# Projections of an attention and expert kernel on quarters of TensorE's array instead of halves

## The chip, the cores and the metric

One core of a Trainium2 chip runs one program. The metric is the time of one execution on the device in microseconds (us). TensorE is called PE below, its weight loads PEld; VectorE is DVE, ScalarE ACT, GpSimd POOL, and SP the engine that issues most transfers.

## The reference

Two layers, cut to what matters. Attention with exponential features (8 batches, 8 heads, 576 positions, 64 dimensions, 128 features), then a routed mixture of 8 experts over the 4608 rows that it gives:

```
def phi(x):                                       # x: batch, head, 576, 64
    proj = einsum('bhsd,df->bhsf', x, w_phi)      # 64 -> 128 features
    proj = proj - max(abs(proj), axis=-1)
    return concatenate([exp(proj), exp(-proj)], -1)
q_p, k_p = phi(q), phi(k)
kv = einsum('bhsf,bhsd->bhfd', k_p, v);  z = sum(k_p, axis=2)
num = einsum('bhsf,bhfd->bhsd', q_p, kv)
den = einsum('bhsf,bhf->bhs', q_p, z) + 1e-06
x = (num / den)                                   # as 4608 rows of 512
logits = x @ w_gate + modality_bias[modality_id]
e = argmax(logits);  gate = softmax(logits)[e]
out = gate * (relu(x @ w1[e]) @ w2[e])
```

The change touches only the product `x @ w_phi` in `phi`.

## The kernel before

**Attention.** The 64 pairs of batch and head are worked in 16 groups of four (`qi` 0 to 15). A group's keys lie in the tile `kt`, 128 partitions of which 64 hold one head and 64 another; its queries lie likewise in `qt`. `w_phi` lies twice in the tile `wp`, once in each half of the partitions. All products here are 4-byte floats, and in the trace each such matmul shows as two records (two passes over its columns), each with a weight load (LDWEIGHTS) of its own.

The projections are made in three helpers of the class Attention, each a sequence of stages:
- `k` (line 461, twice a group): main positions of the keys. Eight matmuls, four times a pair for `a` = 0 and 1, take 64 rows of the array and all 128 columns: weights are 64x128 of `kt`, 128 columns of `wp` move past them. The result goes to the PSUM tile `pk`, of which DVE then takes maxima (line 464) and differences (467), and ACT exponentials (471).
- `e` (lines 481 and 484, once a group): the last 64 positions of the keys and of the queries, four matmuls of 128 moving columns, into two tiles `pe`.
- `q` (line 507, twice a group): main positions of the queries. Two matmuls with `wp` as weights and 512 moving columns, into `pq`. ACT, POOL (an all-reduce over partitions, line 515), DVE and ACT follow.

In the profile these carry the form 64*128 (rows times columns of the array). The two of a pair lie on different halves of the rows and run side by side.

The other products of attention have other forms: `v` sums keys times values into `kvT` on 128*32 (line 534) and its last positions on 64*64 (line 540: four matmuls of 256 moving columns, one on each quarter); `z`, `num` and `den` use 128*32 (575, 592, 599); transposes use 128*128 (554, 581, 674, 683, 692, 698).

**Order.** A list `ORDER`, written by hand, says which stage of which helper of which group comes next; each engine gets its instructions in that order. There are two PSUM buffers of two banks for projections (`pk`, `pq`) and four banks (`pm`) for all else. Loads of later groups are issued when the first stages of K, Q and E have read the tiles.

**Experts.** The class Experts gathers rows (`xg`), transposes them (798), and multiplies with weights that are loaded (`raw`), and split into two parts by ACT (788) and DVE (790): lines 825 and 842. The first of these matmuls stands among the last stages of attention; the last projection stands some 30 us ahead of them.

Of the kernel before, what the change touches and what calls it, by code (L numbers as in the profile page):

```python
# [15 lines left out]
AX = mybir.AxisListType  # L16
PSUM = bass.MemoryType.PSUM
SP, PE, ACT, DVE, POOL = (getattr(mybir.EngineType, e) for e in ("SP", "PE", "Activation", "DVE", "Pool"))

P = 128  # L20
S = 576
# [50 lines left out]
class Route:  # L72
# [28 lines left out]
    def fetch(self, mod, bias):  # L101

        nc, w = self.nc, self.w
        m2 = w.tile([P, NT, 2], I32, name="m2")
        nc.sync.dma_start(m2, mod.bitcast(I32).rearrange("p (t w) -> p t w", w=2))
        bb = w.tile([P, 2, E], F32, name="bb")
        nc.sync.dma_start(bb, bias.rearrange("m e -> (m e)").partition_broadcast(P).rearrange("p (m e) -> p m e", m=2))
        self.raw = m2, bb
# [55 lines left out]
    def group(self, lg, b, pm):  # L164
# [23 lines left out]

        rk = pm.tile([P, 512], F32, tag="pm", name="rk" + n)
        of = self.oh.rearrange("p t e -> p (t e)")  # L190
        for u in range(10):
            nc.tensor.matmul(rk[:, u * E:10 * E], self.one if u else self.U, of[:, 0:(10 - u) * E], start=u == 0, stop=u == 9)
# [146 lines left out]
class Attention:  # L339
# [86 lines left out]
    def load_v(self, qi, lv, vm, vt):  # L426
        nc, q, n = self.nc, self.st[qi], f"{qi}"
        q["va"] = lv.tile([P, 2, 4, P], F32, tag="va", name="va" + n)
        nc.sync.dma_start(q["va"], vm[qi])
        q["vb"] = lv.tile([P, P], F32, tag="vb", name="vb" + n)  # L430
        nc.sync.dma_start(q["vb"], vt[qi])
# [15 lines left out]
    def kp(self, qi, po):  # L447
# [2 lines left out]
            q["kp"] = po.tile([P, 9, 2, 2, P], F32, tag="kp", name=f"kp{qi}")  # L450
        return q["kp"]

    def k(self, qi, u, po, w, pk):


        nc, q, n = self.nc, self.st[qi], f"{qi}_{u}"
        pp = pk.tile([P, 2, 4, P], F32, tag="pk", name="pk" + n)
        for t in range(4):
            for a in range(2):
                r = slice(64 * a, 64 * a + 64)  # L460
                nc.tensor.matmul(pp[:, a, t], q["kt"][r, 4 * u + t], self.wp[r], start=True, stop=True)
        yield
        mk = w.tile([P, 2, 4], F32, tag="mk", name="mk" + n, bufs=2)
        nc.vector.tensor_reduce(mk, pp, AX.X, ALU.max, apply_absolute_value=True)
        yield
        dk = w.tile([P, 2, 4, P], F32, tag="dk4", name="dk" + n)
        nc.vector.tensor_tensor(dk, pp, mk.unsqueeze(3).to_broadcast([P, 2, 4, P]), ALU.subtract)  # L467
        yield
        kp = self.kp(qi, po)[:, 4 * u:4 * u + 4]
        for s, sc in ((0, 1.0), (1, -1.0)):  # L470
            nc.scalar.activation(kp[:, :, :, s, :].rearrange("p t a f -> p a t f"), dk, AF.Exp, scale=sc)  # L471
        yield

    def e(self, qi, po, w, pm):


        nc, q, n = self.nc, self.st[qi], f"{qi}_2"
        pp = [pm.tile([P, 512], F32, tag="pm", name=f"pe{qi}_{a}") for a in range(2)]
        for a in range(2):
            r = slice(64 * a, 64 * a + 64)  # L480
            nc.tensor.matmul(pp[a][:, 0:P], q["kt"][r, 8], self.wp[r], start=True, stop=True)
        for a in range(2):
            r = slice(64 * a, 64 * a + 64)
            nc.tensor.matmul(pp[a][:, P:2 * P].rearrange("p (r s) -> p r s", r=2), self.wp[r], q["qt"][r, :, 512:S], start=True, stop=True)
        yield
        o = self.tail(qi)
        for h in range(2):
            nc.scalar.copy(self.d.rearrange("p (r a) s -> p r a s", a=2)[:, :, h, o:o + 64], pp[h][:, P:2 * P].rearrange("p (r s) -> p r s", r=2))  # L488
        yield
        mk = w.tile([P, 2, 2], F32, tag="me", name="me" + n, bufs=2)  # L490
        for h in range(2):
            nc.vector.tensor_reduce(mk[:, 1, h:h + 1], pp[h][:, 0:P], AX.X, ALU.max, apply_absolute_value=True)
        yield
        kp = self.kp(qi, po)
        nc.scalar.mul(mk[:, 0], mk[:, 1], -1.0)
        for s, sc in ((1, -1.0), (0, 1.0)):
            for h in range(2):
                nc.scalar.activation(kp[:, 8, h, s, :], pp[h][:, 0:P], AF.Exp, bias=mk[:, s, h:h + 1], scale=sc)
        yield

    def q(self, qi, pr, po, w, pq):

        nc, q, n = self.nc, self.st[qi], f"{qi}_{pr}"
        pp = pq.tile([P, 2, 512], F32, tag="pq", name="pq" + n)
        for a in range(2):
            r = slice(64 * a, 64 * a + 64)
            nc.tensor.matmul(pp[:, a], self.wp[r], q["qt"][r, pr, 0:512], start=True, stop=True)
        yield
        d = self.d[:, 2 * pr:2 * pr + 2]
        o = self.main(qi)  # L510
        nc.scalar.copy(d[:, :, o:o + 512], pp)
        yield
        mq = w.tile([P, 2, S], F32, tag="mq", name="mq" + n, bufs=2)
        for a in range(2):
            self.line(nc.gpsimd.partition_all_reduce(mq[:, a], d[:, a], P, bass_isa.ReduceOp.absmax))  # L515
        yield
        nc.vector.tensor_tensor(d, d, mq, ALU.subtract)  # L517
        yield
        if "qp" not in q:
            q["qp"] = po.tile([P, 4, 2, S], F32, tag="qp", name=f"qp{qi}")  # L520
        for i, sc in ((0, 1.0), (1, -1.0)):
            nc.scalar.activation(q["qp"][:, 2 * pr:2 * pr + 2, i, :], d, AF.Exp, scale=sc)  # L522
        yield
# [189 lines left out]
class Experts:  # L713
# [10 lines left out]
    def weights(self, pool, names):  # L724
        for k in names:
            self.W[k] = pool.tile([P, 4, F] if k[1] == "1" else [P, 8, D], F32R, name=k)
# [5 lines left out]
    def entry(self, oi, k, i, top):  # L732

        return self.nc.values_load(oi[0:1, i, k:k + 1], engines=[SP], min_val=0, max_val=top,
                                   skip_runtime_bounds_check_because="the plan makes it within these bounds")
# [28 lines left out]
    def rload(self, r, oi, k, layer):  # L764

        r0 = self.entry(oi, k, 1, (E - 1) * 2 * P)
        for j in range(2):
            self.nc.sync.dma_start(r[2 * layer + j], (self.w1, self.w2)[layer][ds(r0, 2 * P), :]
                                   .rearrange("(p h) c -> p h c", h=2)[:, j])
# [603 lines left out]
```

## Time and profile before

| | |
|---|---|
| time, median of 3 runs | 767.35 us (767.33 to 767.49) |
| the profiled execution | 768.2 us, of which the span shown is 766.1 us |
| PE busy | 742.2 us, 97% of the span |
| DVE busy | 547.4 us, 71% |
| ACT busy | 446.9 us, 58% |
| POOL busy | 294.6 us, 38% |

Busy is the time in which at least one instruction of an engine ran. Attention fills about the first 310 us, the experts the rest. A row of a timeline gives a group's start and the length up to the modelled end of its last matmul; since ends overlap the next group's start, the distance between two starts is the better measure of what a group costs PE.

### The profile page before, as it was taken

The page shows a single profiled execution, that of the slowest core. Times are in us where ns is not written, and L with a number is a line of the kernel's source. Part 1 is how long each engine was busy: PE and PEld are TensorE (multiplying, and loading weights), DVE is VectorE, ACT ScalarE, POOL GpSimd, SP SyncE. Part 2 cuts the span into 40 slices and gives each one's busy share as a digit, 9 for nine tenths or more (in the row PEclk, how much of TensorE's full clock was granted, in tenths as well). Part 3 has the DMA queues.
Part 4 walks back from the last instruction along what each step waited for, and adds up shares of the span by engine and source line. Part 5 has one row for each costly group of instructions (what it writes and reads, how often), then busy time and mean ns, then how long its engine had stood idle before and what let it go on. Part 6 is the DMA issues. An engine that isn't in the chain of part 4 may idle for free. (4 is left out here: it accounts for less than half of the span.)

```text
span 766.1 us, 18619 instructions
## 1 busy us (share of the span) xinstructions
PE 742.2 (97%) x7387; PEld 576.3 (75%) x7387; DVE 547.4 (71%) x832; ACT 446.9 (58%) x677; POOL 294.6 (38%) x199
## 2 busy tenths in 40 slices
PE   8899999999989999999999999999999999999996
PEld 5455655555645555888999988988988999899995
DVE  7898997888778887999765673564646546656653
ACT  5988778787767787545544453444435534554532
POOL 5455345665774884243221231132122123213212
PEclk9999999999999999999999999999999999999999
DMA  8633444447542418699667983847777947786560
GB/s 239 162 96 117 128 128 128 139 114 175 124 113 76 148 19 282 180 238 388 217 207 275 403 321 120 361 162 302 279 289 279 347 165 275 291 340 228 188 241 30
DMA packets 56180, 159.20 MB, mean 208 GB/s; under 512 B 22025, under 2 KB 24205, under 8 KB 43792
## 3 DMA queue, kind: packets, MB, share of 16 engines
q1 hardware_dynamic: 48000, 138.58, 54.2%
q0 software_dynamic: 7760, 18.93, 6.8%
q8 instruction: 62, 1.02, 0.6%
q10 hardware_dynamic: 320, 0.36, 0.2%
q14 instruction: 38, 0.31, 0.1%
HBM read 140.77 MB, written 19.55 MB: 209 GB/s over the span
## 5 line engine op out<-in xcount | busy, mean ns | idle before, releaser
L788 ACT CAST h<-raw 128x1024 fp32r<-128x1024 f32 x148 | 149.6, 1051 | 103.0 <-PE p L842 50.6
L790 DVE TENSOR_TENSOR l<-raw,h 128x1024 fp32r<-128x1024 f32 x148 | 175.6, 1221 | 46.3 <-ACT h L788 35.0
L515 POOL PARTITION_ALL_REDUCE mq<-d x64 | 143.4, 2294 | 104.3 <-ACT d L488 77.3
L825 PE MATMUL p<-xl,h 128*128 128x256 f32 x576 | 163.0, 283 | 0.9 <-issue 0.9
L825 PE MATMUL p<-xh,h 128*128 128x256 f32 x576 | 163.7, 285 | 0.0
L825 PE MATMUL p<-xh,l 128*128 128x256 f32 x576 | 163.0, 284 | 0.0
L746 POOL DMA_INDIRECT xg<-x,me x40 | 56.3, 1406 | 170.7 <-DMA me<-lst 54.2
L825 PEld LDWEIGHTS p<-xh,l 128*128 128x128 f32 x576 | 110.3, 192 | 2.8 <-issue 2.6
L825 PEld LDWEIGHTS p<-xh,h 128*128 128x128 f32 x576 | 110.3, 192 | 1.5 <-issue 1.0
L825 PEld LDWEIGHTS p<-xl,h 128*128 128x128 f32 x576 | 110.4, 192 | 0.9 <-issue 0.4
L831 DVE SCALAR_TENSOR_TENSOR hl<-p,hh 128x512 fp32r<-128x512 f32 x72 | 49.5, 689 | 84.7 <-ACT hh L829 75.1
L842 PE MATMUL p<-h,hh 128*128 128x512 f32 x272 | 104.9, 395 | 0.0
L829 ACT ACTIVATE hh<-p 128x512 fp32r<-128x512 f32 x72 | 42.8, 595 | 106.3 <-PE p L825 91.6
L842 PE MATMUL p<-h,hl 128*128 128x512 f32 x272 | 103.5, 391 | 0.0
L842 PE MATMUL p<-l,hh 128*128 128x512 f32 x272 | 103.4, 390 | 0.0
L522 ACT ACTIVATE qp<-d 128x1152 f32<-128x1152 f32 x64 | 71.1, 1163 | 14.8 <-DVE d L517 13.3
L752 POOL DMA_INDIRECT out_dram<-os,me x34 | 37.5, 1104 | 81.4 <-DVE os L883 62.7
L471 ACT ACTIVATE kp<-dk 128x1024 f32<-128x1024 f32 x64 | 64.7, 1069 | 3.8 <-DVE dk L467 3.7
L534 PE MATMUL kvT<-kp,va 128*32 128x256 f32 x1024 | 61.4, 387 | 5.3 <-DVE xs L663 2.0
L567 DVE TENSOR_TENSOR kp<-kp 128x1024 f32<-128x1024 f32 x48 | 62.7, 1313 | 0.3
L842 PEld LDWEIGHTS p<-h,hl 128*128 128x128 f32 x272 | 51.1, 188 | 10.8
L842 PEld LDWEIGHTS p<-l,hh 128*128 128x128 f32 x272 | 51.1, 188 | 10.3
(259 smaller groups left out, 1114.8 us busy)
## 6 DMA issues: line engine op xcount, KB each, us to landing
raw<-in_w_dram SPq DMA_DIRECT2D x96, 1024.0 KB
qt<-in_qT_dram SPq DMA_DIRECT2D x30, 288.0 KB
va<-in_vm_dram SPq DMA_DIRECT2D x16, 512.0 KB
x<-xs SPq DMA_DIRECT2D x32, 256.0 KB
kt<-in_kT_dram SPq DMA_DIRECT2D x15, 512.0 KB
kt<-in_kT_dram SPq DMA_DIRECT2D x16, 64.0 KB
vb<-in_vt_dram SPq DMA_DIRECT2D x16, 64.0 KB
x<-xs_l SPq DMA_DIRECT2D x8, 128.0 KB
```

Source lines behind the costliest of these rows:

```text
L471: nc.scalar.activation(kp[:, :, :, s, :].rearrange("p t a f -> p a t f"), dk, AF.Exp, scale=sc)
L515: self.line(nc.gpsimd.partition_all_reduce(mq[:, a], d[:, a], P, bass_isa.ReduceOp.absmax))
L522: nc.scalar.activation(q["qp"][:, 2 * pr:2 * pr + 2, i, :], d, AF.Exp, scale=sc)
L534: nc.tensor.matmul(pt[pr][32 * c:32 * c + 32], va[:, pr, t, 32 * c:32 * c + 32], kp[:, pr * 4 + t, c // 2, :, :], start=t == 0, stop=False ...
L567: nc.vector.tensor_tensor(kv4[:, :, t], kv4[:, :, t], kv4[:, :, u], ALU.add)
L746: g = self.nc.gpsimd.indirect_dma_start(xg, None, self.x[:rows, :], IndirectOffsetOnAxis(ix.bitcast(U32), 0), bounds_check=rows - 1, oob_i ...
L788: nc.scalar.copy(h, r)
L790: nc.vector.tensor_tensor(l, r, h, ALU.subtract)
L825: nc.tensor.matmul(pp[:, j], a[:, cc, f], b[:, cc], start=i == 0, stop=i == 11)
L829: nc.scalar.activation(self.HH[:, sl], pp, AF.Relu)
L831: nc.vector.scalar_tensor_tensor(self.HL[:, sl], pp, 0.0, self.HH[:, sl], ALU.max, ALU.subtract)
L842: nc.tensor.matmul(pp, a[:, f, tk], b[:, f], start=i == 0, stop=i == 23)
```

## The change

A new helper `quarters` takes the place of the matmul in `k`, `e` and `q`. It splits the 128 columns of the weights into two halves and issues one matmul for each, on the quarter of the array that begins at row 64a and column 64c. Each writes 64 partitions of the output instead of 128. The moving operand is the same for both. The moving columns stay as they were (128 for keys and both tails, 512 for the main queries).

```
+    def quarters(self, o, w, m, a):
+        for c in range(2):
+            self.nc.tensor.matmul(o[64 * c:64 * c + 64], w[:, 64 * c:64 * c + 64], m, start=True, stop=True, tile_position=(64 * a, 64 * c))
...
-                nc.tensor.matmul(pp[:, a, t], q["kt"][r, 4 * u + t], self.wp[r], start=True, stop=True)
+                self.quarters(pp[:, a, t], q["kt"][r, 4 * u + t], self.wp[r], a)
...
-            nc.tensor.matmul(pp[a][:, 0:P], q["kt"][r, 8], self.wp[r], start=True, stop=True)
+            self.quarters(pp[a][:, 0:P], q["kt"][r, 8], self.wp[r], a)
...
-            nc.tensor.matmul(pp[a][:, P:2 * P].rearrange("p (r s) -> p r s", r=2), self.wp[r], q["qt"][r, :, 512:S], start=True, stop=True)
+            self.quarters(pp[a][:, P:2 * P].rearrange("p (r s) -> p r s", r=2), self.wp[r], q["qt"][r, :, 512:S], a)
...
-            nc.tensor.matmul(pp[:, a], self.wp[r], q["qt"][r, pr, 0:512], start=True, stop=True)
+            self.quarters(pp[:, a], self.wp[r], q["qt"][r, pr, 0:512], a)
```

The projections become 768 matmuls instead of 384. On DVE, ACT, POOL and SP nothing moves. On PE the sequence of groups stays; only the projections' rows change. An early place on PE (the second group's last products of `v`, then a projection of keys) reads before:

```order
L534 MATMUL kvT_1_333<-kp_267,va_194 32x256 x16
L540 MATMUL kvT_0_282<-kp_267,vb_196 64x256 x2
L540 MATMUL kvT_1_333<-kp_267,vb_196 64x256 x2
L461 MATMUL pk_1_359<-wp,kt_198 128x128 x8
L534 MATMUL kvT_0_378<-kp_330,va_204 32x256 x16
```

and with the change (the sizes are partitions times columns of the output):

```order
L539 MATMUL kvT_1_371<-kp_291,va_194 32x256 x16
L545 MATMUL kvT_0_306<-kp_291,vb_196 64x256 x2
L545 MATMUL kvT_1_371<-kp_291,vb_196 64x256 x2
L456 MATMUL pk_1_397<-wp,kt_198 64x128 x16
L539 MATMUL kvT_0_424<-kp_368,va_204 32x256 x16
```

The eight matmuls of `pk` are sixteen now, and have the form of the two rows of line 545 ahead of them. A run of projections a little later on PE, between products of other forms, reads before:

```order
L461 MATMUL pk_1_772<-wp,kt_433 128x128 x8
L481 MATMUL pe_0_784<-wp,kt_433 128x128
L481 MATMUL pe_1_785<-wp,kt_433 128x128
L484 MATMUL pe_0_784<-qt_434,wp 128x128
L484 MATMUL pe_1_785<-qt_434,wp 128x128
L507 MATMUL pq_1_796<-qt_434,wp 128x512 x2
L592 MATMUL pn_0_805<-qp_502,kv_709 32x448 x8
```

and with the change:

```order
L456 MATMUL pk_1_854<-wp,kt_481 64x128 x16
L456 MATMUL pe_0_874<-wp,kt_481 64x128 x2
L456 MATMUL pe_1_875<-wp,kt_481 64x128 x2
L456 MATMUL pe_0_874<-qt_482,wp 64x128 x2
L456 MATMUL pe_1_875<-qt_482,wp 64x128 x2
L456 MATMUL pq_1_890<-qt_482,wp 64x512 x4
L597 MATMUL pn_0_901<-qp_560,kv_789 32x448 x8
```

In PE's order there are 47 such runs of projections, before and after; 10 of them stand directly behind the matmuls of line 540, and 3 directly ahead of them.

## Rows read from the trace of the kernel before

**Rows 1.** Busy time by stretch; columns PE, PEld, DVE, ACT, POOL (instructions), clock, DMA.
```profile
0.00:26.00 26.00, 21.26 (x209) 12.54 (x213) 19.18 (x43) 17.18 (x28) 10.48 (x14) 0.93 0.89 244
26.00:280.00 254.00, 245.97 (x3603) 145.04 (x3595) 218.87 (x330) 198.91 (x341) 155.61 (x83) 1.00 0.44 118
280.00:310.00 30.00, 27.72 (x448) 15.79 (x448) 23.46 (x39) 22.07 (x38) 13.59 (x9) 1.00 0.57 195
310.00:766.00 456.00, 447.24 (x3139) 402.94 (x3137) 285.93 (x424) 208.72 (x271) 114.90 (x95) 1.00 0.71 256
```

**Rows 2.** PE's waits, 26 to 310 us: total, times, longest.
```profile
PE pl L592 <- issue: 2.4, 5, 1.0
PE kvT L534 <- DVE xs L663: 2.0, 2, 1.1
PE pl L592 <- DVE zg L585: 1.6, 1, 1.6
PE zp L575 <- ACT xt L608: 1.5, 1, 1.5
PE kvT L534 <- ACT kp L471: 0.6, 1, 0.6
```

**Rows 3.** Timeline of PE, 40 to 75 us: start, length, line, tiles, form, records.
```profile
40.84 1.13 PE L507 MATMUL pq<-qt,wp 64*128 64x512 f32 x4
41.80 1.06 PE L461 MATMUL pk<-wp,kt 64*128 64x128 f32 x16
42.79 1.93 PE L534 MATMUL kvT<-kp,va 128*32 128x256 f32 x32
...
48.54 1.13 PE L507 MATMUL pq<-qt,wp 64*128 64x512 f32 x4
49.60 1.71 PE L592 MATMUL pn<-qp,kv 128*32 128x448 f32 x16
...
52.00 0.62 PE L599 MATMUL pl<-qp,zg 128*32 128x128 f32 x16
52.44 1.69 PE L599 MATMUL pd<-qp,zg 128*32 128x448 f32 x16
54.05 1.16 PE L461 MATMUL pk<-wp,kt 64*128 64x128 f32 x16
55.05 0.39 PE L481 MATMUL pe<-wp,kt 64*128 64x128 f32 x4
55.27 0.39 PE L484 MATMUL pe<-qt,wp 64*128 64x128 f32 x4
55.49 1.03 PE L507 MATMUL pq<-qt,wp 64*128 64x512 f32 x4
...
67.26 1.16 PE L461 MATMUL pk<-wp,kt 64*128 64x128 f32 x16
68.35 0.66 PE L540 MATMUL kvT<-kp,vb 64*64 64x256 f32 x8
68.94 1.08 PE L592 MATMUL pl<-qp,kv 128*32 128x128 f32 x32
...
73.95 1.03 PE L507 MATMUL pq<-qt,wp 64*128 64x512 f32 x4
74.90 0.66 PE L683 MATMUL xp<-ident,xt 128*128 128x128 f32 x4
```

**Rows 4.** Two lines' weight loads: records, shortest/median/longest ns, first and last start.
```profile
L461 PEld LDWEIGHTS pk<-wp,kt x512: 182/188/334, 5.3 to 277.8; 64*128 64x128 f32 x171
L540 PEld LDWEIGHTS kvT<-kp,vb x128: 129/131/133, 18.6 to 289.7; 64*64 64x64 f32 x128
```

**Rows 5.** Busy time by stretch, where the granted clock fell.
```profile
20.00:22.00 2.00, 0.97 (x16) 0.78 (x14) 2.00 (x3) 2.00 (x3) 0.00 (x0) 1.00 0.90 237
22.00:24.00 2.00, 1.24 (x12) 0.60 (x16) 1.97 (x3) 2.00 (x5) 0.00 (x0) 0.57 0.97 233
```

**Rows 6.** Busy time by stretch, where the experts begin.
```profile
320.00:360.00 40.00, 39.38 (x247) 35.27 (x246) 38.08 (x108) 21.18 (x26) 16.84 (x18) 1.00 0.96 280
```

## The prediction

> **What bounds the kernel now.** I first read the busy time by stretch [rows 1]. The reader is to see two things. In the stretch that holds almost all projections (26 to 280 us) PE is busy 245.97 of 254 us, DVE 218.87, ACT 198.91, POOL 155.61: PE sets the pace, and DVE, at 86%, has some 35 us to spare but is not far. Behind 310 us, where the experts are, PE is busy 447.24 of 456 us, so an attention that ends earlier moves the end of the program, if the experts' inputs come earlier too. Second, PE's waits [rows 2]: the five costliest groups add up to 8.1 us in 284 us, none over 1.6 us long; 2.4 us have no releaser that the profile shows, the rest is for DVE or ACT. Third, the timeline of PE [rows 3], where the distance between starts gives what a run of one form costs.
>
> **What a projection costs PE.** A query block `pq` that stands alone between other forms takes 49.60 - 48.54 = 1.06 us; one that opens a run and is followed by `pk` of the same form 41.80 - 40.84 = 0.96; one that closes a run 74.90 - 73.95 = 0.95. So opening a run costs 0.11, closing it 0.10, and the block itself 0.85. Key blocks say the same: alone 68.35 - 67.26 = 1.09, opening 55.05 - 54.05 = 1.00, closing 42.79 - 41.80 = 0.99; itself 0.90, which is eight steps of 0.112 (two matmuls, one on each half of the rows, make two steps of 128 columns). The closing cost is that of a change of form: inside the run `pk`, `pe`, `pe`, `pq` at 54.05 it is absent (the two `pe` take 0.22 each, two steps of 0.11) [rows 3].
>
> What is the opening cost? The block of line 540, which already works on quarters, tells. It takes 68.94 - 68.35 = 0.59. It moves 256 columns, half of a `pq` block's 512, so its stream is 0.425; the closing costs 0.10; 0.065 is left for the opening, against 0.105 on average with 128 columns of weights [rows 3]. So I read the opening cost as the first weight load, which nothing covers. The records of the loads agree: the shortest of line 461, 128 columns, is 182 ns, that of line 540, 64 columns, 129; they differ by 0.053 us [rows 4].
>
> **The change, part by part.**
>
> 1. *The streams.* Twice as many matmuls, each with half of the output. If four quarters run side by side as two halves did, the streams are as long as before. Line 540 supports it: four quarters of 256 columns would take 0.85 and not 0.425 if they ran two by two, and its block would cost over 1.0 instead of 0.59 [rows 3].
>
> 2. *The step.* A step of 128 columns is 0.112 now. The trace has no run of quarters with 128 columns. The nearest row is `pl` on 128*32, four matmuls side by side as here, 128 columns: 16 records between 52.00 and 52.44, four steps of 0.110 [rows 3]. An upper bound without loss is today's 0.112, a lower one an eighth of the `pq` stream, 0.85/8 = 0.106. There are 320 steps (128 pairs in `k`, 32 in `e`, two passes each). I take 0.110: 320 x 0.002 = 0.6 us, between 0 and 1.9. The 64 passes of `q` stay at 0.427.
>
> 3. *Opening a run.* 47 runs, of which 10 stand behind line 540. For the other 37: 37 x 0.053 = 2.0 us; by the starts (0.105 - 0.065 = 0.04) it is 1.5, which I keep as the lower bound.
>
> 4. *Line 540 as a neighbour.* Projections then have its form, 64*64. Where a run follows it (10 times) both its closing cost, 0.10, and the run's whole opening cost, 0.105, should vanish, since the next load then goes under the running stream as it does inside a run: 10 x 0.205 = 2.05 us. Where a run stands ahead of it (3 times), 0.10 + 0.065 vanish: 0.5 us. If a change of form costs as much even here, this part gives only the shorter opening, 10 x 0.053 = 0.5.
>
> 5. *Issue.* Twice as many matmuls go through PE's queue. `pl` shows 16 records in 0.44 us, 0.0275 each [rows 3], and a step of quarters needs four in 0.110, the same rate. The Trainium skill ("TensorE: Matmul & The Clock Gate", section "Wait — 56ns, not 53.3ns?") has a rule that speaks against the change: with hardware decode off, some 62 ns per matmul in the sequencer, the bound where array work per matmul is shorter. By it a step would take an estimated 4 x 62 = 248 ns and the sum would be a loss of some 44 us. `pl` at 27.5 ns per record does not agree with it, so it is not a term here.
>
> Nothing moves on the other engines, no transfer is added, and PSUM buffers and their waits stay.
>
> Sum on PE: 0.6 + 2.0 + 2.05 + 0.5 = 5.15 us. The first 26 us do not count: PE is busy only 21.26 of 26 there [rows 1], behind loads and first results. Three runs lie there, one of them behind line 540: 2 x 0.053 + 0.205 = 0.3 us off. **4.85 us of PE time remain.**
>
> **How much reaches the end.** Each of the waits for DVE or ACT [rows 2] is a place where a neighbour was later than PE. What PE saves between its product and that wait, it waits longer there. The rows name eleven such waits, some 25 us apart; what is saved well ahead of one moves the neighbour too, since its own work starts from PE's earlier products. How far back that reaches no row says; I choose 30% as lost and 70% as kept, 3.4 us, and keep half and all for the range. Late next are the same ones: `kvT` behind line 663, `pl` behind 585, `zp` behind 608. The profiled execution took 768.2 us (766.1 of span, 2.1 around it), so 764.8; the median of the runs shown is 0.85 lower, so **764.0 us**, 0.4% faster. Its own range is 0.5 to 1 of 4.85, 762.5 to 764.9.
>
> **Rivals.**
>
> - *The neighbourhood of line 540 gives nothing* (a change between two blocks costs the same whatever the form). For it: no row shows 64*64 followed by 64*64 of another line. Against: all changes within 64*128 and from `pl` to `pd` within 128*32 are free of it [rows 3]. Sum 0.6 + 2.0 + 0.5 - 0.15 = 2.95, kept 2.05: 765.3.
> - *The rhythm of DVE and ACT takes it all.* For it: the waits already there [rows 2], and DVE, now at 86%, would be at 88%. Against: DVE has some 35 us of idle time in the stretch [rows 1], so no backlog of it lasts. Or the experts' loads take it: DMA is at 0.96 of its time from 320 to 360 us [rows 6], and if weights or gathered rows do not come earlier, PE waits there. Against: nearly all of these loads are issued when earlier steps are done, so they move with PE. 766.5 to 767.5, no change to be measured.
> - *The step of quarters is longer* (slower). Each step starts four weight loads and four streams; where the two quarters of one half of the rows share a path for loads or moving data, the step grows. The gains outside the steps are 4.85 - 0.6 = 4.25 us, over 320 steps 0.013: from 0.125 per step on the change loses. At 0.150 it costs 320 x 0.038 = 12.2, net some 8 us slower: 775. A queue that feeds PE more slowly than `pl` shows has the same price per step; of the 0.07 below I give it 0.01. (The rule of the Trainium skill in part 5 would be its far end.) Against: line 540's first loads would then show, and its opening cost 0.065 is less than one load of 128 columns [rows 3].
> - *Quarters of one half of the rows do not run side by side at all* when the weights change from step to step, as line 540 never does. Then 32 x 0.90 + 32 x 0.85 + 16 x 0.44 = 63 us more on PE: about 830.
>
> **How the numbers follow.** Chances: the forecast 0.62, line 540 without effect 0.14, no change 0.13, longer step 0.07, not side by side 0.04. What a measurement here can tell from no change is about 0.2%, 1.5 us. Faster by more: nearly all of the first case and most of the second, 0.72; within it 0.17; slower 0.11. The range reaches down to 761.5, where the step falls to 0.107 and all is kept (1.6 + 4.25 = 5.85 us off the median), and up to 767.2, which takes in the second case and most of the third and leaves out the two slow ones.
>
> **What the profile after would show.** A key block that stands alone at 1.02 instead of 1.09; a query block alone at 1.01 instead of 1.06; line 540 followed by a projection at some 0.48 instead of 0.59, with no gap between; 32 records in eight steps of 0.110 in `pk`; first matmul of the experts some 3 us earlier; PE's waits up by 1 to 2 us between 26 and 310 us. What would make it wrong: steps above 0.12; waits that grow by more than 3 us; or the granted clock. It fell once, to 0.57 of full between 22 and 24 us, after PE had been busy 0.97 of 2 us [rows 5]. If PE, being earlier, idles as long at another place, it may fall there too, and a stretch at the lower of the two levels (1.2 instead of 2.4 GHz) costs about what it lasts at half speed; one such fall would take back half of the gain.

## The result, and the profile after

In the measurement that the prediction was made for, the changed kernel took **775.53 us** (median of four runs, 772.72 to 777.21), the kernel before 767.42 (four runs, 767.33 to 767.9). The ratio is 1.0089, 95% interval 1.0066 to 1.0112: 0.9% slower, where 0.4% faster was forecast. It did not stay so. Measured three more times beside the kernel before, in three other jobs (a job is a set of runs on one chip; the three are on three chips), the same program came out at 0.9966 (0.9933 to 0.9999), 1.0017 (1.0002 to 1.0033) and 0.9971 (0.9947 to 0.9994). These ratios are not the quotients of the medians, which are 1.0106 for the first measurement and then 0.9990, 1.0006 and 0.9978. The ratio 0.9966 leaves out the change's slowest run, 775.15 us, as disturbed, and keeps one of 775.16 us of the kernel before, so it isn't clear of 1.00. So two questions have to be kept apart: what the change does, and what the first measurement saw.

Busy time by stretch of the changed kernel's first profile (columns as in [rows 1]):

```profile
0.00:26.00 26.00, 20.94 (x337) 11.70 (x337) 19.71 (x44) 17.59 (x30) 11.09 (x14) 1.00 0.90 242
26.00:280.00 254.00, 240.68 (x4086) 137.76 (x4086) 212.65 (x315) 191.84 (x330) 148.08 (x79) 0.99 0.45 118
280.00:310.00 30.00, 28.51 (x503) 17.19 (x495) 23.27 (x44) 22.77 (x38) 18.41 (x12) 1.00 0.45 137
310.00:772.00 462.00, 454.23 (x3244) 406.59 (x3242) 291.84 (x432) 214.70 (x281) 114.54 (x97) 1.00 0.71 257
```

From 26 to 280 us every engine did less in the same time than before [rows 1], DVE 212.65 us of work instead of 218.87, although nothing was taken from DVE: the program is behind. The experts' first matmul (line 830) starts at 316.88 us; before it was 309.54. In the experts about 1 us came back.

PE's waits from 26 to 310 us in the same profile, to be laid beside [rows 2] (the change moved later lines by five):

```profile
PE pe L456 <- issue: 3.6, 10, 1.0
PE kvT L539 <- DVE xs L668: 2.1, 2, 1.2
PE zp L580 <- ACT xt L613: 1.3, 1, 1.3
...
PE pk L456 <- issue: 0.5, 2, 0.3
PE pn L597 <- issue: 0.2, 1, 0.2
```

All waits together are 14.2 us, where the kernel before has 9.7. Idle time without a releaser, called unnamed idle below, has grown from 2.4 to 4.3 us and now stands on the projections. The named waits have grown too, from 7.3 to 9.9 us, in many small ones.

The timeline of PE, 40 to 70 us, is what answers to [rows 3] (line 456 is the new helper, 545 is 540 of before):

```profile
40.04 1.09 PE L456 MATMUL pq<-qt,wp 64*64 64x512 f32 x8
40.95 1.05 PE L456 MATMUL pk<-wp,kt 64*64 64x128 f32 x32
41.93 1.93 PE L539 MATMUL kvT<-kp,va 128*32 128x256 f32 x32
...
47.72 1.09 PE L456 MATMUL pq<-qt,wp 64*64 64x512 f32 x8
48.74 1.71 PE L597 MATMUL pn<-qp,kv 128*32 128x448 f32 x16
...
53.21 1.10 PE L456 MATMUL pk<-wp,kt 64*64 64x128 f32 x32
54.13 0.40 PE L456 MATMUL pe<-wp,kt 64*64 64x128 f32 x8
54.35 0.40 PE L456 MATMUL pe<-qt,wp 64*64 64x128 f32 x8
54.57 1.04 PE L456 MATMUL pq<-qt,wp 64*64 64x512 f32 x8
...
67.62 1.10 PE L456 MATMUL pk<-wp,kt 64*64 64x128 f32 x32
68.54 0.61 PE L545 MATMUL kvT<-kp,vb 64*64 64x256 f32 x8
69.08 0.65 PE L597 MATMUL pl<-qp,kv 128*32 128x128 f32 x16
```

The blocks cost what was forecast. `pq` opening a run: 40.95 - 40.04 = 0.91 (0.96 before). `pq` alone: 48.74 - 47.72 = 1.02 (1.06). `pk` opening a run: 0.92 (1.00). `pk` ahead of `kvT` on quarters: 68.54 - 67.62 = 0.92 (1.09), and that `kvT` 0.54 (0.59). The quarters are not the loss.

It was made behind 168 us. From 75 to 168 us DVE's instructions start within 0.2 us of before. At 203 us they are 4.0 late, at 224 to 229 us 7, and so it stays to the experts. In the timeline of PE these two places look like this (last column: idle time ahead, and what ended it; "issue": nothing that the profile shows):

```profile
199.61 1.10 PE L456 MATMUL pk<-wp,kt 64*64 64x128 f32 x32
200.53 0.40 PE L456 MATMUL pe<-wp,kt 64*64 64x128 f32 x4
201.20 0.34 PE L456 MATMUL pe<-wp,kt 64*64 64x128 f32 x2 [0.27 <-issue]
...
201.97 0.43 PE L456 MATMUL pe<-qt,wp 64*64 64x128 f32 x4 [0.32 <-issue]
203.38 0.45 PE L456 MATMUL pe<-qt,wp 64*64 64x128 f32 x3 [0.98 <-issue]
203.76 1.08 PE L597 MATMUL pl<-qp,kv 128*32 128x128 f32 x32
...
222.08 1.35 PE L456 MATMUL pk<-wp,kt 64*64 64x128 f32 x27
223.68 0.47 PE L456 MATMUL pk<-wp,kt 64*64 64x128 f32 x3 [0.25 <-issue]
...
225.18 0.44 PE L456 MATMUL pe<-wp,kt 64*64 64x128 f32 x5 [0.29 <-issue]
225.92 0.27 PE L456 MATMUL pe<-wp,kt 64*64 64x128 f32 x1 [0.30 <-issue]
...
226.66 0.43 PE L456 MATMUL pe<-qt,wp 64*64 64x128 f32 x2 [0.27 <-issue]
227.38 0.38 PE L456 MATMUL pe<-qt,wp 64*64 64x128 f32 x2 [0.29 <-issue]
```

A tail (two `pe` of eight records) takes 203.76 - 200.53 = 3.23 us instead of 0.44 at 54.13. At 225 us a handful of matmuls comes every 0.74 us, and then nothing: PE has its operands and idles for want of instructions, or so the rhythm looks; no row shows its queue. Both times POOL issues the routing's scatters of list entries (line 202), here from 197.8 and from 218.8 us, one each 1.27 us. The 2.4 us "issue" of before [rows 2] lie beside scatters too.

Behind the second place the granted clock (the last column but two) fell to the lower of its two levels, 1.2 instead of 2.4 GHz:

```profile
224.00:226.00 2.00, 1.13 (x14) 0.49 (x12) 1.64 (x2) 1.59 (x2) 1.39 (x3) 1.00 0.29 43
226.00:228.00 2.00, 1.45 (x10) 0.61 (x11) 0.00 (x0) 0.00 (x0) 1.59 (x2) 1.00 0.38 121
228.00:230.00 2.00, 1.83 (x11) 0.44 (x12) 0.00 (x0) 0.00 (x0) 0.00 (x0) 0.74 0.10 9
230.00:232.00 2.00, 2.00 (x25) 1.49 (x19) 0.00 (x0) 0.05 (x1) 0.00 (x0) 0.50 0.70 18
232.00:234.00 2.00, 2.00 (x69) 1.99 (x62) 1.31 (x3) 2.00 (x7) 0.15 (x1) 0.90 0.70 69
```

That is 3.4 us at half speed, at most 1.7 us lost. The kernel before had such a fall at 22 us [rows 5]; this profile has none there.

From this come three theories. **A:** while POOL issues these scatters, PE is supplied badly; quarters, with twice as many instructions, lose by it. **B:** any earlier PE upsets the written order (stores, DVE meeting POOL). **C:** quarters are slower in themselves; the rows above speak against it.

### The profile page after: what moved, and what is told of

It is laid out like the page before. It is cut to its first block, busy times and chain, and to the rows that moved or that the text cites. A ratio compares the mean times of both kernels' runs of the same rounds, so it can differ in the third digit from the quotient of the medians.

```text
span 772.4 us, 20155 instructions
## 1 busy us (share of the span) xinstructions
PE 744.4 (96%) x8155; PEld 573.2 (74%) x8155; DVE 547.5 (71%) x832; ACT 446.9 (58%) x677; POOL 292.1 (38%) x199
## 5 line engine op out<-in xcount | busy, mean ns | idle before, releaser
L751 POOL DMA_INDIRECT xg<-x,me x40 | 53.4, 1336 | 173.3 <-PE pt L803 62.2
```

Of the source, the lines that this page charges most:

```text
L751: g = self.nc.gpsimd.indirect_dma_start(xg, None, self.x[:rows, :], IndirectOffsetOnAxis(ix.bitcast(U32), 0), bounds_check=rows - 1, oob_i ...
```

## The experiments

In all, sixteen runs in four jobs; the kernel before ran beside them in each (medians 766.63, 768.17, 762.99 and 767.5 us; its single runs spread from 764.2 to 774.2, 764.1 to 775.2, 760.8 to 763.9 and 765.7 to 774.7).

**Without the scatters.** In both kernels:

```diff
-            self.listed.append(apart(self.tc, "lst", self.line(nc.gpsimd.indirect_dma_start(
-                self.lst, IndirectOffsetOnAxis(de[:, t:t + 1].bitcast(U32), 0), meta[:, t, :], None), False)))
```

> The change, with the 36 scatters of the routing list left out (lines 202: the list then holds only its padding, the experts gather and scatter nothing, so only attention's time is to be read, by the start of the first expert matmul). Theory A (PE is fed its instructions too slowly while GpSimd issues these scatters, and quarters, with twice as many instructions per us, lose there): PE's unnamed idle time between 168 and 290 us, 4.3 us with scatters, falls under 1 us, the three jumps at 184, 201 and 223 us go, and the first expert matmul starts 0 to 4 us earlier than in the same kernel with halves. Theory B (any earlier PE upsets the written order, by waits for stores, DVE and ACT; instructions do not matter): it starts 3 to 7 us later than with halves, as it did with scatters (316.9 against 309.5 us).

> The kernel before with the same 36 scatters left out (list and experts as in the run with quarters): the other half of that comparison. Theory A: the unnamed idle time of PE, 2.4 us between 168 and 290 us, goes too, so the first expert matmul comes 1 to 3 us earlier than 309.5 us, from POOL's free time perhaps more. Theory B: 309 to 310 us.

Quarters: 762.58 us (761.71 to 762.91, ten runs). Halves: 763.73 (762.76 to 764.76, twelve runs). Neither profile has any unnamed idle of PE from 26 to 310 us. The medians differ by 1.15 us. The experts begin at 299.64 and 301.36 us, 1.7 us apart, but nothing of this distance is made from 27 to 167 us. The same two instructions of DVE, first in e2 (halves), then in e1 (quarters):

```profile
28.17 1.22 DVE L465 TENSOR_TENSOR dk<-pk,mk 128x1024 f32<-128x1024 f32 x1
167.38 1.21 DVE L565 TENSOR_TENSOR kp<-kp 128x1024 f32<-128x1024 f32 x1
```

```profile
27.01 1.22 DVE L470 TENSOR_TENSOR dk<-pk,mk 128x1024 f32<-128x1024 f32 x1
166.26 1.21 DVE L570 TENSOR_TENSOR kp<-kp 128x1024 f32<-128x1024 f32 x1
```

Quarters are 1.16 us ahead at 27 us and 1.12 at 167 us; the other 0.6 us come behind that. At 27 us the four profiles of the change without further edits (the first, e5, e9, e15) lie up to 2.2 us apart, so one pair doesn't show that this lead is the change's. The spread of the runs shrinks without the scatters: standard deviations of 0.38 and 0.53 us, beside 3.0 for the kernel before on that chip. The experts begin 8.2 us earlier in e2 than in the first profile of before, far more than its 2.4 us of unnamed idle; what else a scatter costs is seen below, in e11. So far theory A holds in its first half, and theory C falls. (The experts gather nothing in these two, so their totals aren't to be compared with the others.)

**Parts of the change.** e3: line 456's helper in `q` alone, halves in `k` and `e`. e4: halves in `q`. e6: halves in `e`. The edit is always this, at the place named:

```diff
-            self.quarters(pp[:, a], self.wp[r], q["qt"][r, pr, 0:512], a)
+            nc.tensor.matmul(pp[:, a], self.wp[r], q["qt"][r, pr, 0:512], start=True, stop=True)
```

> Quarters only for the main queries (32 blocks of 512 columns, 128 matmuls instead of 64), halves in keys and tails. These blocks need only 16 instructions in 0.85 us more, so the feed is not tight. Theory A: no loss, 766 to 768 us, with some of the gain from shorter openings eaten by DVE and ACT. Theory B: part of the loss, 769 to 773 us, since PE is earlier here too (about 1.9 us of work saved).

> Quarters only for keys and both tails (640 matmuls instead of 320, 128 columns each), halves for the main queries. Theory A: nearly all of the loss, 773 to 777 us, with unnamed idle time of PE of 3 to 6 us at the scatters. Theory B: part of the loss, by how much PE is earlier: 769 to 773 us.

> Quarters in the key and main query blocks, halves again in the tails. Behind the change two of the three places where PE idled without a named reason stand in the tails (`pe`). Theory A in its narrow form (tails on quarters are the piece that PE is fed too slowly for while POOL issues the scatters): at most 1 us of unnamed idle, 764 to 767 us. Theory A in its wide form (any dense stretch of 128-column matmuls that meets a series of scatters, whichever block it is): unnamed idle of 2 us or more stays, on `pk`, `pl` or `pn`, and the time is between 766 and 776. Theory B (the written order is upset by whatever comes earlier): first matmul of the experts 4 us or more later than before, without unnamed idle.

e3 took 767.54 us, ratio 0.9993 (0.9967 to 1.0019); e4 765.04, 0.997 (0.9943 to 0.9998); e6 766.87, 0.9967 (0.9935 to 0.9999). Theory A had expected e4 to be as slow as the change; it wasn't. Unnamed idle turned up on other lines: 2.2 us in e4 (`kvT`, `pl`), 1.8 in e6 (`kvT`), 0.5 in e3. It belongs to no block of the change. (The whole change did not run in the job of e3 and e4. e6 lies between the two forms of theory A: more than 1 us of unnamed idle, but less than 2.)

**The change again, and the kernel before against itself**, without an edit.

> The changed kernel as it is, beside the kernel before on one chip, with the three kernels below. If the loss belongs to the change (theories A and B alike), it is again 0.5 to 1.1% slower than before, 771 to 777 us. If it is a matter of how the runs happened to fall on the first chip, the interval of its ratio takes in 1.00.

> The changed kernel again, in another job, beside the control e12. Theory A (each execution loses 0 to 8 us at random where POOL's scatters meet PE, before and after alike, and the change itself saves what its blocks save): 0.2 to 0.5% faster than before, single runs spread over 763 to 775 us. Theory C (the change loses 0.9%, as in the first measurement): 1.005 or more.

> The kernel before, against itself: what an interval is worth here when nothing is changed. Its ratio takes in 1.00; single runs from 764 to 775 us. Its profile is a second execution of the same program: theory A expects that its DVE starts agree with the first profile within 0.5 us up to about 195 us and differ by 2 to 8 us behind 235 us, with the difference made where scatters are issued.

> The changed kernel again, in a fourth job. By the three before it (+0.9%, -0.3%, +0.2%) its sign goes with the job: theory A2 (random losses of both kernels) expects 0.995 to 1.005, theory A1 (quarters lose more in whatever job the losses are large) expects 1.002 or more where the kernel before is above 766 us, and 1.000 or less where it is at 763.

The change: 767.41 us (763.52 to 775.15), 763.42 (760.92 to 767.64) and 765.8 (763.96 to 770.01), with the ratios given at the top. The kernel before against itself: 762.8, ratio 1.0002 (0.9992 to 1.0012). e5 did not repeat the loss: what was to be explained isn't a property of the program alone. The profile of e9 shows this best, since it is another execution of the very program of the first one. The timeline of PE at the same two places:

```profile
197.17 1.10 PE L456 MATMUL pk<-wp,kt 64*64 64x128 f32 x32
198.09 0.40 PE L456 MATMUL pe<-wp,kt 64*64 64x128 f32 x8
198.31 0.40 PE L456 MATMUL pe<-qt,wp 64*64 64x128 f32 x8
198.64 1.08 PE L597 MATMUL pl<-qp,kv 128*32 128x128 f32 x32
...
216.99 1.05 PE L456 MATMUL pk<-wp,kt 64*64 64x128 f32 x32
217.86 0.39 PE L456 MATMUL pe<-wp,kt 64*64 64x128 f32 x4
218.92 0.33 PE L456 MATMUL pe<-wp,kt 64*64 64x128 f32 x2 [0.67 <-ACT xt L613]
...
219.10 0.48 PE L456 MATMUL pe<-qt,wp 64*64 64x128 f32 x6
219.51 1.71 PE L597 MATMUL pn<-qp,kv 128*32 128x448 f32 x16
```

The tail at 198.09 takes 0.55 us, not 3.23. The four scatters stand in the same place relative to it: 195.37 us here, 2.72 ahead of the tail; 197.80 there, 2.73 ahead. So it isn't a matter of this alignment either: one execution loses at that place, the next doesn't. DVE's starts in the first profile lie behind those of e9 by 1.6 us at 168 us, 2.8 at 183, 6.6 at 201, 10 at 226 and 11 when the experts begin (316.88 against 305.82); 1.3 us of it stand at 42 us already, and near 217 us, where e9 waits in its turn, it is down to 3.1. That is nearly the whole difference of the two spans, 772.4 and 760.7 us. The profiled run of e5, 775.15 us, is as slow as the first measurement again: its experts begin at 317.59 us, with 2.8 us of unnamed idle and a mean granted clock of 0.96 from 168 to 290 us.

e9 and e12 are two executions of one job with at most 0.4 us of unnamed idle: the experts begin at 305.82 us with quarters, at 307.20 with halves. These 1.4 us aren't the change's worth either: the quarters are 2.7 us ahead at 27 us, 2.5 at 167, and lose 1.1 of that later.

The expectations of e9 and e12 failed: the change was not faster in that job, no run reached 768 us, and DVE's starts in e12 lie 1.1 us behind the first profile of before already at 27 us, then 1.5 ahead of it at 235. In e15, theory A1 expected 1.002 or more, and 0.9971 came.

**Where the scatters stand.** Four routing steps moved in the written order, so that the series of scatters come apart; in the changed kernel and in the one before, the latter twice:

```diff
+for i, j in ((599, 624), (592, 611), (586, 599), (530, 516)):
+    ORDER.insert(j, ORDER.pop(i))
```

> The changed kernel with four routing steps moved in the written order, so that the two long series of scatters (4 from 198 us, 7 from 219 us) come apart with other work between. Nothing is left out. Theory A (the loss is made where a series of scatters meets a dense stretch of PE): unnamed idle below 1 us, 763 to 767 us. Theory B (stores and collisions of DVE, ACT and POOL at shifted phases): the places at 170, 184 and 202 us stay, 770 to 776 us.

> The same four moves in the kernel before, as the control for the run above. Theory A: the unnamed idle of 2.4 us on `pl` goes, so up to 2 us faster than before, 764 to 767 us; quarters with the same order are 0 to 2 us faster than this one. Theory B: 766 to 769 us, the same as before, and quarters with the same order are slower than this one.

> The kernel before with the four moved routing steps again, in another job. If the order itself makes the place of the scatters harmless: again faster than before, 0.993 to 0.998, with a smaller standard deviation. If the gain in its first job came from the large losses of that job's kernel before: 0.998 to 1.002 in a job whose kernel before is at 763 us.

Quarters: 766.91 us, 0.9984 (0.9955 to 1.0013). Halves: 763.54, 0.9948 (0.9921 to 0.9974), and again 764.9, 0.9955 (0.9933 to 0.9978). Unnamed idle 0.8, 0.6 and 1.5 us, now on `zp`. For halves the move works, in two jobs, and it leaves the projections alone; the change itself was clear of noise below 1.00 in one job of four (e15). The expectation that quarters gain as much failed: in the same job and order they are 3.4 us slower than halves. Their profiles begin the experts at 305.89 and 305.54 us, so what shows in the medians isn't in these two executions; I have no cause for it.

**What of a scatter does it.** In the changed kernel, e10 writes the list with plain DMAs of the same bytes from SP's queue (unsorted); e11 keeps POOL busy instead (nine memsets for each scatter).

```diff
+            r0 = 128 * (9 * b + t)
+            self.listed.append(nc.sync.dma_start(self.lst[r0:r0 + 128, :], meta[:, t, :]).ins)
```

```diff
+            for _ in range(9):
+                self.line(nc.gpsimd.memset(self.busy, 0.0), False)
```

> The changed kernel; each of the 36 scatters of list entries is a plain write of the same 1 KB from SP's queue to fixed rows of the list (the list is then not sorted by expert; the experts gather other rows). It has the small writes to memory without the indirect DMA on POOL. If PE is fed badly because of the indirect DMAs that POOL issues: as in the run without scatters, no unnamed idle of PE and the standard deviation of the runs about 0.5 us. If the many small packets to memory are enough: unnamed idle of 1 us or more, standard deviation 1.5 us or more.

> The changed kernel; each of the 36 scatters is replaced by nine memsets on POOL of about the same total length (0.9 us), so that POOL's rhythm stays and the DMA goes (the list then holds padding alone, and the experts gather no rows). Theory A: as without scatters, 762 to 764 us, standard deviation 0.5 us, no unnamed idle. Theory B (POOL's time, or its collisions with DVE, upsets the rhythm): spread and unnamed idle stay.

e10: 767.25 us (767.06 to 767.66, five runs). e11: 769.57 (768.84 to 769.94, four runs). Both totals hold an altered expert part; what counts is that neither has unnamed idle, and that both are steady, with standard deviations of 0.23 and 0.46 us, where e9 in the same job has 1.95. That points to the indirect DMA, and not to POOL's time or the small writes, as what makes PE idle without a reason. It is no proof: each is one profile, e12 has no unnamed idle with all its scatters, and the kernel before spread by only 0.76 us in this job. But POOL's time has a price of its own. The waits of DVE, 26 to 310 us, in e11 and then in e1:

```profile
DVE d L523 <- POOL mq L521: 7.9, 7, 2.1
```

```profile
DVE d L520 <- POOL mq L518: 2.1, 3, 1.1
```

The experts begin at 305.73 us in e11 and at 299.64 in e1. POOL's all-reduces come behind the memsets, and DVE waits 5.8 us longer for them. Theory B has that much right; my expectation of 762 to 764 us for e11 was wrong by it.

**Scatters doubled**, the second into a list that nobody reads, in both kernels:

```diff
+            apart(self.tc, "lst2", self.line(nc.gpsimd.indirect_dma_start(
+                self.lst2, IndirectOffsetOnAxis(de[:, t:t + 1].bitcast(U32), 0), meta[:, t, :], None), False))
```

> The changed kernel with each of the 36 scatters issued a second time, to a second list that nobody reads (nothing is left out; POOL gets some 36 x 1.1 us = 40 us more work). Theory A1 (PE is fed badly while scatters are issued, and quarters, with twice as many instructions, lose more by it): slower than halves with doubled scatters (e14) by 2 us or more. Theory A2 (scatters hold up halves and quarters alike, at random): within 1.5 us of e14. Both: spread of 2 us or more and unnamed idle of PE above 1 us.

> The kernel before with the same doubled scatters. Theory A (A1 and A2): slower than before by 2 to 10 us, standard deviation as large as that of before or larger, unnamed idle of PE above 1 us. If scatters are not the reason: within 1 us of before, since POOL had some 90 us of idle time in the stretch from 26 to 280 us.

Quarters 800.63 us, 1.0421 (1.0377 to 1.0465); halves 801.92, 1.0446 (1.0396 to 1.0496). Far more than expected, and alike: quarters don't lose more (A1 falls, A2 holds). But little of it is unnamed idle, 2.0 us in e13 and none in e14. The waits of DVE, 26 to 338 us, in e14:

```profile
DVE d L519 <- POOL mq L517: 18.0, 8, 5.3
DVE dn L618 <- ACT xt L638: 12.8, 5, 3.3
DVE xs L665 <- DMA x<-xs: 6.6, 2, 6.2
```

As in e11 it is POOL's time ahead of its all-reduces: the first line stands at 2.8 us in e12, so some 15 of the 30 us by which the experts begin later (337.37 against 307.20). The third stands at 2.9 us in e12. And the granted clock, 1.00 in e12 from 168 to 290 us, was lower in e14:

```profile
168.00:290.00 122.00, 103.13 (x1402) 58.64 (x1400) 84.70 (x131) 76.68 (x134) 88.11 (x62) 0.93 0.58 108
```

How the 30 us divide among these was not measured. So the doubling was a poor test of the supply.

## Why the prediction was wrong

*The streams, the step, the opening of a run, line 540 as a neighbour:* right, each within about 0.02 us per block. The step is (0.92 - 0.05)/8 = 0.109 by `pk` at 53.21, 0.110 forecast. `kvT` of line 545 followed by `pq` takes 198.38 - 197.90 = 0.48 us in the first profile, as forecast. The rival of the longer step, the one of quarters that don't run side by side and the one of line 540 without effect are refuted by the same rows. That the longer step was priced at 775 us, close to the 775.53 measured, is chance.

*How much reaches the end:* this step failed. I chose 70% of 4.85 us, 3.4; without the scatters the medians give 1.15, about a quarter of the 4.85, and from 27 to 167 us the profiles give nothing. (With the scatters even the sign is not settled: the four ratios run from 0.9966 to 1.0089.) The busy time of 26 to 168 us shows where it stays, first before, then after:

```profile
26.00:168.00 142.00, 140.76 (x2097) 83.36 (x2090) 124.85 (x182) 115.41 (x198) 75.03 (x35) 1.00 0.42 117
```

```profile
26.00:168.00 142.00, 137.46 (x2458) 80.31 (x2455) 124.62 (x180) 114.98 (x197) 74.22 (x35) 1.00 0.44 118
```

PE needs 3.3 us less for what DVE, ACT and POOL do in the same time as before, and its waits there, nearly all for DVE or ACT, grow from 1.1 to 4.1 us (from e2 to e1 likewise, 1.1 to 4.2). DVE comes no earlier by it: from 27 to 167 us the first profile of the change falls back by 0.5 us against before, e1 against e2 by 0.04. This is the rival of the rhythm, which had 0.13, and I had argued against it from DVE's 35 us of idle time: idle time on a neighbour doesn't help where the neighbour's chain, and not its sum, is what PE waits for. My 30% came from eleven waits between 26 and 310 us, of which [rows 2] show five. A forecast of 0.4% would have looked right beside the 0.3% of e15, and that would have been luck.

*Issue, and the time of before taken as given:* this step failed too; unnamed idle is part of what turned the sign in the first measurement. I took `pl` at 27.5 ns per record as proof that PE's queue is fast enough, and it is, on average. I passed over the other reading of the same profile, 2.4 us on `pl` that no releaser explains [rows 2]: a supply that fails now and then. In e1, e2, e10 and e11 it is gone with the indirect DMAs, and e9 shows that it comes and goes between executions of one program. Two signs that I had named came true in the first profile: waits grew by 4.5 us, more than 3, and the granted clock fell at another place, 229 us. The three runs of before within 0.2 us, and then four within 0.6, made its time look sharp to a tenth of a per cent; in three of the four later jobs its runs spread over 9 to 11 us. My chances allowed 1.5 us for the measurement.

*What stays open.* Why all four runs of the change lost in the first job while none of the four of before did: in the three later jobs the change had 2 of 36 runs above 771 us, so chance is a poor answer, and nothing here tells the job's part from the program's. How an indirect DMA holds PE up was not shown. The traces have one lead. Instruction packets of 16 KB on DMA queue 8, of which a kernel with halves moves 62 and one with quarters 68 (so they are very likely PE's), take 0.99 us by the median of the first profile. In each of the 14 profiles with scatters, two to seven of them between 26 and 310 us take 2.0 us or more, up to 3.6; in the four without (e1, e2, e10, e11) none takes more than 1.9. But slow packets and losses don't match one to one: the first profile has packets of 2.7 us at 200.0 and 229.8 us, close to its losses, and e9 has four of 2.3 to 2.8 us and loses little.

## What to carry to other kernels

A saving on the engine that sets the pace reaches the end only where its neighbours' chains let it: look whether the stretch's other engines would do their work sooner, not whether they have idle time left. Idle time without a releaser on the pacing engine is a finding to follow before any term of 0.5 us is summed: here the executions of one program lay up to 11 us apart at the end of attention, several times the change's effect, and 4 us of that were such idle time. And a gain of a few tenths of a per cent is measured by repeating both kernels in more than one job; four tight runs each gave an interval that the next three jobs left.

## What the runs showed of the hardware

- Two executions of one program, with the same instructions in the same places, differed by 3.23 against 0.55 us in one tail of 16 matmul records, and by 11 us at the end of attention. Without the 36 indirect DMAs (0.99 us each on POOL by the median) the standard deviation of the runs fell from 3.0 us to 0.4 to 0.5.
- Four quarters of the array with 128 columns and new weights for each step run side by side at 0.109 us per step; the first load of a run is 0.05 us shorter than with 128 columns of weights, and between line 545 and a projection of the same form no cost of a change is left (0.48 us for the block, where 0.59 was needed).
- 36 more indirect DMAs on POOL, 36 to 37 us of its time, made the program 33 to 34 us longer, though POOL was idle for 34 of the 122 us from 168 to 290 us (e14): some 15 us are DVE's longer waits for the all-reduces behind them. The granted clock was 0.93 in that stretch, and 1.00 with the scatters of before (e12).
- After PE had been busy only 1.13 and 1.45 us in two stretches of 2 us, the granted clock fell to 0.50 for 3.4 us (first profile, 229 us).
- Instruction packets of 16 KB on DMA queue 8, between 26 and 310 us, took up to 3.6 us in kernels with the scatters, and at most 1.9 us without them.
